# Two product orders and three moved tasks in a retention and mixture-of-experts kernel

## The chip, the cores and the metric

The kernel runs on one core of a Trainium2 chip. The core has a matrix engine (TensorE, PE in the profile, with its weight loads as PEld), VectorE (DVE), ScalarE (ACT), GpSimd (POOL) and SyncE (SP, which only issues DMAs here). The metric is the device time of one execution in microseconds. Lower is better. The time before is a median of three runs.

## The reference

A retention layer (8 sequences of 576 positions, 8 heads of 64) feeds a top-1 mixture of 8 experts, all in float32.

```python
ret = scale * (q @ k.T) * Dmat          # Dmat[i, j] = gamma ** (i - j), lower triangle
x = (ret @ v)                           # reshaped to N=4608 tokens of D=512
expert_idx = np.argmax(xn @ en.T / tau, axis=1)
gate_w = softmax(...)[chosen expert]
for e in range(8):
    mask = expert_idx == e
    h = np.maximum(x[mask] @ w1[e], 0.0)            # 512 -> 1024
    out[mask] = gate_w[mask, None] * (h @ w2[e])    # 1024 -> 512
```

## The kernel before

The first part of the program (up to about 170 us) computes the retention, routes every token to its expert and writes the token rows and the gates to DRAM. Then the experts follow one after the other. Each expert has room for 640 tokens, held as CT = 5 tiles of 128. A float32 operand is split into a high and a low part, and each product is made of three matmuls (high by high, high by low, low by high).

For experts 1 to 7 the **first product** (x @ w1) is done in blocks. A two-by-two block scheme with 7 products (numbered n = 1 to 7) stands in place of 8, for each of four column groups i = 0 to 3, so an expert has 28 **block products** `(n, i)`. Each is six matmuls of 128 rows by 288, 304 or 320 columns; the width is chosen at run time by how many tokens the expert has, which is why the built program holds each product three times behind branches (L1264, L1267), of which one is run. The tuple `ORDER` gives the order of the 28, and its place in that order is called k below (k = 1 is the first).

The sums of the scheme are made in PSUM. Products 1, 6, 7 and 4 of a column group all accumulate into one bank, `Y[i]`, in this order. After 1, 6 and 7 the function `follow` has ScalarE copy the running sum from the bank to SBUF (L1279), because the scheme needs each of these partial sums. So product 7 may not start to write the bank before the copy after product 6 has read it. Product 2 has a bank `W[i]` and products 5 and 3 share a bank `Z[i]`. VectorE adds `W` and `Z` onto the copies (L1275, `add`), ScalarE applies the relu (L1224) and VectorE makes the low part (L1217).

```python
if n in (1, 6, 7):
    nc.scalar.copy({1: ya, 6: yb, 7: yc}[n][:, :HC], Y[i][:, :HC])
```

The copies land in the tiles `ys[0]` to `ys[4]`. The same tiles hold the output rows of the expert before, so a copy also waits until GpSimd's scatter of those rows has been done.

The **second product** (h @ w2, function `mm2`, L1349) runs over the five tiles: 24 matmuls of 128 by 512 each, then ScalarE scales the rows by the gate (L1375) and GpSimd scatters them to the output (`put_rows`, L1309, an indirect DMA). The fifth tile of experts 1 to 6 is special (`fitted`): where at most 64 tokens are left for it, its rows are packed, and one pair of passes over the packed tile `ht` (a part of the tile `w0s`) replaces the three. `both_parts` makes that packing with four VectorE copies from `hs` (L1331). Where nothing is left, the tile is left out.

All other work is spread over these two stages by hand. `mm1_plan(e)` says which tasks are written after which block product k, and `mm2_plan(e)` which are written at which third of which tile (index 3 * tile + third). Every engine runs its own instructions strictly in the order in which they are written, and waits on semaphores for what it needs. The tasks that matter here:

- `gather_gates(n, a0, a1)`: GpSimd fetches the gates of tiles a0 to a1 of expert n from DRAM (L380, one indirect DMA for each tile). They are read first when the second product of expert n is scaled.
- `gather`: GpSimd fetches the token rows of the expert after next (L366).
- `xjoin`, `xsums`, `xhigh`, `xlow`: ScalarE and VectorE prepare the x blocks of the next expert during the second product (L415 on ScalarE; L426, L432, L433, L454 on VectorE).
- `w1sum`, `w1hi`, `w1lo`, `w2hi`, `w2lo`: the sums and splits of the weights (L1175, L1149, L1152).
- `add_low`: GpSimd scatters the rows of the packed tile a second time with an add (L1309, `sidx`), after k = 10.

Of the kernel before, what the change touches and what calls it, by code (L numbers as in the profile page):

```python
# [29 lines left out]
CT = 5  # L30
# [65 lines left out]
def retention_moe(ctx: ExitStack, tc: tile.TileContext, qk, kn, v0s, vs, w1, w2, head, cst, out):  # L96
# [263 lines left out]
    def fitted(e, i):  # L360
        return i == CT - 1 and 0 < e < NE - 1
# [189 lines left out]
    with ExitStack() as att:  # L551
# [3 lines left out]
        a1 = att.enter_context(tc.tile_pool(name="a1", bufs=1))  # L555
# [551 lines left out]
    with ExitStack() as moe:  # L1107
# [164 lines left out]
        def follow(n, i):  # L1272
# [23 lines left out]
                highs.append(settle(yb, i, 1))  # L1296

        ORDER = (
# [3 lines left out]
        )  # L1302
# [87 lines left out]
        def mm2_plan(e):  # L1390
            n = e + 1
            own, sums = slice(0, 1), slice(1, 3)
            if n == NE:
                return {0: [(count_beyond,)], 3: [(half_rows,)]}
            plan = {
                0: [(xjoin, n, 0)],
                1: [(xsums, n, 0), (xhigh, n, 0, own), (xlow, n, 0, own), (xjoin, n, 1), (w1sum, n, 0), (xhigh, n, 0, sums)],
                2: [(w1hi, n, 0, True), (xsums, n, 1), (xlow, n, 0, sums), (xhigh, n, 1, own), (w1lo, n, 0, True)],
                3: [(xjoin, n, 2), (xlow, n, 1, own), (xhigh, n, 1, sums)],
                4: [(w1hi, n, 0, False), (xsums, n, 2), (xlow, n, 1, sums), (w1lo, n, 0, False)],  # L1400
                5: [(xhigh, n, 2, own), (xjoin, n, 3), (xlow, n, 2, own), (xhigh, n, 2, sums)],
                6: [(w1sum, n, 1), (xhigh, n, 3, own), (xsums, n, 3), (w1hi, n, 1, True), (xjoin, n, 4)],
                7: [(w1lo, n, 1, True), (xlow, n, 3, own), (xhigh, n, 3, sums), (xsums, n, 4), (xlow, n, 2, sums)],
                8: [(xhigh, n, 4, own), (xlow, n, 4, own), (xlow, n, 3, sums), (xhigh, n, 4, sums), (w1hi, n, 1, False)],
                9: [(xlow, n, 4, sums), (w1lo, n, 1, False)],
                10: [(w1sum, n, 2)],
                11: [(w1hi, n, 2, True), (w1lo, n, 2, True)],
                12: [],
            }
            if n + 1 < NE:  # L1410
                for i in range(CT):
                    plan[(2, 4, 8, 9, 11)[i]].append((gather, n + 1, i))
            if fitted(e, CT - 1):
                plan[9].insert(1, (both_parts,))
            for k, a0, a1 in ((2, 0, 2), (5, 2, 4), (9, 4, CT)):
                plan[k].insert(0, (gather_gates, n, a0, a1))
            if n + 1 < NE:
                plan[12].append((xturn, n + 1, 0))
            if e == 0:
                plan[0] = [(xturn, 1, 4)] + plan[0]  # L1420
            return plan

        def mm1_plan(e):
            n = e + 1
            plan = {
                2: [(w2hi, e, 0)],
                3: [(w2lo, e, 0)],
                5: [(w1hi, e, 2, False)],
                6: [(w1lo, e, 2, False), (w1sum, e, 3)],
                12: [(w1hi, e, 3, True)],  # L1430
                13: [(w1lo, e, 3, True)],
                14: [(w1hi, e, 3, False)],
                15: [(w1lo, e, 3, False)],
                18: [(w2hi, e, 1)],
                19: [(w2lo, e, 1)],
                21: [(w2hi, e, 2)],
                22: [(w2lo, e, 2)],
            }
            if n < NE:
                plan[10] = [(xturn, n, 3)]  # L1440
                plan[16] = [(xturn, n, 1)]
                plan[24] = [(xturn, n, 2)]
                plan[28] = [(xturn, n, 4)]
            return plan
# [13 lines left out]
        for f, ps in zip(PAIRS, first):  # L1458
            mm1_out(f, 0, ps)

        plan = {
            4: [(w2hi, 0, 0)],
            5: [(w2lo, 0, 0)],
            6: [(xprep, 0, 3), (xprep, 0, 4), (gates_exp,)],
            7: [(w2hi, 0, 1)],
            8: [(gates_sum,), (w2lo, 0, 1)],
            9: [(w2hi, 0, 2), (gather, 1, 3), (gather, 1, 4)],
            10: [(gates_out,), (w2lo, 0, 2), (xturn, 1, 0)],
            11: [(w2hi, 0, 3)],
# [9 lines left out]
        for e in range(NE):  # L1479
            if e:  # L1480
                plan = mm1_plan(e)
                for k, (n, i) in enumerate(ORDER, 1):
                    product(e, n, i)
                    follow(n, i)
                    if k == 10 and fitted(e - 1, CT - 1):
                        add_low(e - 1)
                    if k < len(ORDER):
                        run_tasks(plan, k)
                highs.pop()()
                w2hi(e, 3)  # L1490
                lows.pop()()
                w2lo(e, 3)
                held.pop()()
                run_tasks(plan, len(ORDER))
            plan = mm2_plan(e)
            for i in range(CT):
                if (e, i) == (0, 2):
                    load_left()
                if e * CT + i == NA - 2:
                    ntile = nc.values_load(ovt[0:1, 0:1], min_val=0, max_val=NO)  # L1500
                mm2(e, i, lambda k: run_tasks(plan, 3 * i + k))
# [196 lines left out]
```

## Time and profile before

| | |
|---|---|
| median of three runs | 551.64 us (551.02 to 553.75) |
| the profiled execution | 551.17 us |
| its span, first to last instruction | 549.1 us |
| PE busy in the span | 541.6 us, 99% |
| PEld, DVE, ACT, POOL busy | 89%, 76%, 69%, 46% |
| granted TensorE clock | 1.000, all of the span |

The profiled execution takes 2.1 us more than its span, which is time ahead of the first and behind the last instruction. A busy share is an average over stages with different limits. TensorE's matmuls are pipelined and their ends are modelled, so a row can reach past the start of the next one. The time that matters is the distance from the start of one group of matmuls to the start of the next: what it holds beyond the usual pace of that group is a stall, also where the row shows a smaller idle time.

### The profile page before, as it was taken

To read this page: it belongs to the slowest core of one execution; us is meant where nothing else is said; L and a number is where in the kernel's file an instruction comes from. 1 tells how busy PE (TensorE), PEld (TensorE's weight loads), DVE (VectorE), ACT (ScalarE), POOL (GpSimd) and SP (SyncE) were. 2 spreads that over 40 slices of the span, in tenths; PEclk is the share of its full clock that TensorE was granted. 3 is DMA by queue.
4 is the path that set the end of the run, shared out by engine and by line. 5 is a ranking of instruction groups with operands and counts; after the bars stand their busy time and mean duration, and the time that the engine had idled before them with its cause. 6 is when DMAs were issued, how large, how long until landed. Compare 5 with 4: busy or idle time off the path is not lost. (4 is left out here: it accounts for less than half of the span.)

```text
span 549.1 us, 13547 instructions
## 1 busy us (share of the span) xinstructions
PE 541.6 (99%) x5051; PEld 489.4 (89%) x5051; DVE 419.9 (76%) x975; ACT 377.4 (69%) x700; POOL 250.9 (46%) x239
## 2 busy tenths in 40 slices
PE   9999999999999999999999999999999999999996
PEld 8898988989898899889988987998898899889985
DVE  4856788798876957995897889689888958976810
ACT  1257454547758859977896898789789868957511
POOL 6773435553463751285057318704731851334022
PEclk9999999999999999999999999999999999999999
DMA  9999999978458474847556655675665565632111
GB/s 325 407 383 369 371 330 356 378 275 274 160 186 206 161 203 117 166 146 185 159 167 168 164 163 175 183 159 161 184 164 157 173 174 154 137 135 64 66 39 50
DMA packets 81974, 109.79 MB, mean 200 GB/s; under 512 B 43094, under 2 KB 44538, under 8 KB 81888
## 3 DMA queue, kind: packets, MB, share of 16 engines
q1 hardware_dynamic: 71920, 86.24, 51.4%
q0 software_dynamic: 8560, 20.16, 11.9%
q10 hardware_dynamic: 1408, 2.17, 1.1%
q8 instruction: 63, 1.03, 0.7%
q14 instruction: 23, 0.19, 0.1%
HBM read 80.27 MB, written 21.51 MB: 185 GB/s over the span
## 5 line engine op out<-in xcount | busy, mean ns | idle before, releaser
L1349 PE MATMUL m<-w2s,hs 128*128 128x512 f32 x552 | 127.2, 389 | 0.0
L1349 PEld LDWEIGHTS m<-w2s,hs 128*128 128x128 f32 x552 | 103.4, 188 | 21.3
L1309 POOL DMA_INDIRECT out<-y,sid x41 | 45.7, 1115 | 166.1 <-ACT y L1375 134.1
L1349 PE MATMUL a<-w2s,hs 128*128 128x512 f32 (+1 forms) x360 | 78.8, 375 | 0.0
L1349 PEld LDWEIGHTS a<-w2s,hs 128*128 128x128 f32 x360 | 64.2, 188 | 11.9
L366 POOL DMA_INDIRECT raw<-xd,gid x40 | 42.9, 1073 | 19.4 <-issue 9.3
L1224 ACT ACTIVATE hs<-y 128x320 fp32r<-128x320 f32 x84 | 39.2, 473 | 13.1 <-DVE y L1275 12.5
L415 ACT COPY raw<-raw 128x1024 uint16<-128x1024 uint16 x35 | 47.7, 1363 | 0.0
L734 POOL TENSOR_TENSOR kt<-kt,cs 128x512 f32<-128x512 f32 x28 | 28.4, 1044 | 42.1 <-DMA kt<-kn 42.1
L380 POOL DMA_INDIRECT gt<-gd,gid x34 | 39.0, 1146 | 17.2 <-issue 9.7
L1152 DVE TENSOR_TENSOR w2s<-raw,w2s 128x1024 fp32r<-128x1024 f32 x32 | 39.1, 1222 | 8.3 <-ACT w2s L1149 8.2
L1275 DVE TENSOR_TENSOR y<-a,y 128x320 f32<-128x320 f32 x53 | 25.5, 486 | 26.0 <-issue 11.4
L1217 DVE SCALAR_TENSOR_TENSOR hs<-y,hs 128x320 fp32r<-128x320 f32 x84 | 42.3, 510 | 3.3 <-ACT hs L1224 1.3
L1255 PE MATMUL m<-xsb,w0s 128*128 128x288 f32 (+2 forms) x270 | 43.8, 300 | 0.1
L1255 PE MATMUL a<-xsb,w0s 128*128 128x288 f32 (+2 forms) x270 | 43.6, 301 | 0.2 <-ACT y L1279 0.2
L1255 PEld LDWEIGHTS a<-xsb,w0s 128*128 128x128 f32 x270 | 39.2, 188 | 0.4 <-ACT y L1279 0.4
L1255 PEld LDWEIGHTS m<-xsb,w0s 128*128 128x128 f32 x270 | 39.2, 188 | 0.3 <-DVE hs L1217 0.3
L1375 ACT ACTIVATE y<-m,gt 128x512 f32<-128x512 f32 x26 | 17.8, 686 | 31.0 <-PE m L1349 31.0
L408 ACT COPY raw<-raw 128x1024 uint16<-128x1024 uint16 x35 | 36.6, 1045 | 0.0
L1149 ACT CAST w2s<-raw 128x1024 fp32r<-128x1024 f32 x32 | 33.4, 1043 | 2.4 <-DMA raw<-w 2.4
L753 POOL TENSOR_TENSOR qkt<-qkt,gsb 128x384 f32<-128x384 f32 x32 | 31.3, 1008 | 6.5 <-issue 4.2
L454 DVE TENSOR_TENSOR xsb<-raw,xsb 128x128 fp32r<-128x128 f32 x70 | 30.4, 484 | 0.0
(274 smaller groups left out, 1216.9 us busy)
## 6 DMA issues: line engine op xcount, KB each, us to landing
raw<-w SPq DMA_DIRECT2D x64, 512.0 KB
qkt<-qk SPq DMA_DIRECT2D x28, 576.0 KB
xd<-y SPq DMA_DIRECT2D x36, 256.0 KB
vt<-vs SPq DMA_DIRECT2D x7, 1152.0 KB
kt<-kn SPq DMA_DIRECT2D x7, 1024.0 KB
qkt<-qk ACTq DMA_DIRECT2D x4, 288.0 KB
qkt<-qk SPq DMA_DIRECT2D x4, 288.0 KB
out<-y,sid POOLq DMA_INDIRECT x41
```

The lines of the kernel that those rows point to most:

```text
L366: nc.gpsimd.indirect_dma_start(out=t[:, XO : XO + DM], out_offset=None, in_=xd[:rows, :], in_offset=bass.IndirectOffsetOnAxis(ap=gid[:, a ...
L380: nc.gpsimd.indirect_dma_start(out=g[:, i : i + 1], out_offset=None, in_=gd[:, :], in_offset=bass.IndirectOffsetOnAxis(ap=ids, axis=0),)
L408: nc.scalar.copy(far.rearrange("p (h n) -> p h n", h=2), near.rearrange("p (n h) -> p h n", h=2))
L415: nc.scalar.copy(far.bitcast(U16).rearrange("p (n h) -> p h n", h=2), near.rearrange("p (h n) -> p h n", h=2))
L753: nc.gpsimd.tensor_tensor(out=q, in0=q, in1=gsb[:, p, :], op=ALU.mult)
L1149: nc.scalar.copy(hi, u)
L1152: nc.vector.tensor_tensor(out=lo, in0=u, in1=hi.bitcast(F32), op=ALU.subtract)
L1217: nc.vector.scalar_tensor_tensor(out=lo, in0=part(src), scalar=0.0, in1=hi.bitcast(F32), op0=ALU.max, op1=ALU.subtract)
L1224: nc.scalar.activation(hi, part(src), AF.Relu)
L1255: nc.tensor.matmul(ps[:, :n_cols], w[:, ws, ka, d * P : (d + 1) * P], xop(kx, xsp)[:, d, :n_cols], start=(n in (1, 2, 5) and d == 0 and k ...
L1309: put = nc.gpsimd.indirect_dma_start(out=out.rearrange("t (k n) -> (t k) n", k=k), out_offset=bass.IndirectOffsetOnAxis(ap=rows, axis=0), ...
L1349: nc.tensor.matmul(ps[:, :step], rows[f // NPR][:, f % NPR] if rows is ht else rows[:, f], w[:, ws, f, n : n + step], start=(m == 0), stop ...
```

## The change

```diff
         ORDER = (
-            (1, 0), (2, 0), (5, 0), (1, 1), (6, 0), (2, 1), (5, 1), (7, 0), (6, 1), (1, 2),
+            (1, 0), (2, 0), (5, 0), (1, 1), (2, 1), (5, 1), (6, 0), (7, 0), (6, 1), (1, 2),
...
             if fitted(e, CT - 1):
-                plan[9].insert(1, (both_parts,))
-            for k, a0, a1 in ((2, 0, 2), (5, 2, 4), (9, 4, CT)):
+                plan[0].append((both_parts,))
+            for k, a0, a1 in ((2, 0, 2), (5, 2, 4), (9, 4, CT))[1 if e else 0 :]:
                 plan[k].insert(0, (gather_gates, n, a0, a1))
...
             if n < NE:
                 plan[10] = [(xturn, n, 3)]
+                plan[11] = [(gather_gates, n, 0, 2)]
                 plan[16] = [(xturn, n, 1)]
```

Three things move; nothing is added or taken away.

**The order of the block products**, in all seven experts. `(6, 0)` goes from place 5 to place 7, behind `(2, 1)` and `(5, 1)`. The first six products now each start on a bank of their own. `(7, 0)` stays at place 8. On TensorE (last expert, the copies of 304 columns, with the semaphores of the engines that a row waits for; `a3` is the bank `Y[0]`, `m2` is `W[1]`, `m0` is `Z[1]`, `a1` is `Y[1]`) places 5 to 9 read before:

```order
L1255 MATMUL a3_67<-xsb_2531,wsa_2532 128x304 [waits Activation_49]
L1255 MATMUL a3_67<-xsb_2531,wsa_2532 128x304 x5
...
L1255 MATMUL m2_70<-xsa_94,w0s_89 128x304 x6
...
L1255 MATMUL m0_68<-xsb_2531,w0s_89 128x304 x2
L1255 MATMUL m0_68<-xsb_2531,w0s_89 128x304 [waits DVE_49]
L1255 MATMUL m0_68<-xsb_2531,w0s_89 128x304 x3
...
L1255 MATMUL a3_67<-xsb_2531,wsa_2532 128x304 [waits Activation_49]
L1255 MATMUL a3_67<-xsb_2531,wsa_2532 128x304 x5
...
L1255 MATMUL a1_65<-xsb_2531,w0s_89 128x304 x6
```

and with the change:

```order
L1255 MATMUL m2_70<-xsa_94,w0s_89 128x304 x6
...
L1255 MATMUL m0_68<-xsb_2531,w0s_89 128x304 [waits Activation_49]
...
L1255 MATMUL m0_68<-xsb_2531,w0s_89 128x304 [waits DVE_49]
L1255 MATMUL m0_68<-xsb_2531,w0s_89 128x304 x3
...
L1255 MATMUL a3_67<-xsb_2531,wsa_2532 128x304 [waits Activation_49]
L1255 MATMUL a3_67<-xsb_2531,wsa_2532 128x304 x5
...
L1255 MATMUL a3_67<-xsb_2531,wsa_2532 128x304 [waits Activation_49]
L1255 MATMUL a3_67<-xsb_2531,wsa_2532 128x304 x5
...
L1255 MATMUL a1_65<-xsb_2531,w0s_89 128x304 x6
```

The two products on bank `a3`, `(6, 0)` and `(7, 0)`, had two products of other banks between them and now follow each other. The wait of the second is for ScalarE's copy of the first.

On ScalarE the copies move along. At the same place in the last expert it had `y1` (the copy after `(1, 1)`), `y2` (after `(6, 0)`), the cast of `w1hi`, the relu of `y1` and `y0` (after `(7, 0)`):

```order
L1279 COPY y1_85<-a1_65 128x320 [waits DMASW1_49,PE_49]
L1279 COPY y2_86<-a3_67 128x320 [waits DMASW4_49,PE_49,Activation_49]
L1149 CAST w0s_89<-wsum_2534 128x1024
...
L1224 ACTIVATE hs_2530<-y1_85 128x5x64 [waits DVE_49]
L1279 COPY y0_84<-a3_67 128x320 [waits PE_49,Activation_49]
```

and it now has:

```order
L1279 COPY y1_85<-a1_65 128x320 [waits DMASW1_49,PE_49]
L1149 CAST w0s_89<-wsum_2534 128x1024
L1224 ACTIVATE hs_2530<-y1_85 128x5x64 [waits DVE_49]
L1279 COPY y2_86<-a3_67 128x320 [waits DMASW4_49,PE_49,Activation_49]
...
L1279 COPY y0_84<-a3_67 128x320 [waits PE_49,Activation_49]
```

The cast and the relu now stand ahead of the copy of `y2`.

**VectorE's row copies** (`both_parts`, experts 1 to 6) go from the fourth tile of the second product to the first third of the first tile. On VectorE, at the head of the second product of expert 1, behind the last low parts of the first product (`hs`) and ahead of the first sums of the next x (`raw`):

```order
 L1152 TENSOR_TENSOR w2s<-raw_77,w2s 128x1024
 L1217 SCALAR_TENSOR_TENSOR hs<-y_84,hs 128x5x64
+L1331 COPY w0s<-hs 128x8x32 x4
 L426 TENSOR_TENSOR raw_78<-raw_78 128x256
 L432 TENSOR_TENSOR raw_78<-raw_78 128x128
```

The four copies have been put between `hs` and the x sums.

**GpSimd's gathers of the first two gates** of experts 2 to 7 (two indirect DMAs each, twelve in all) go from the head of the second product to the block products ahead of it, after k = 11. The other three gates of an expert stay.

## Rows read from the trace of the kernel before

**Rows 1.** The page: busy time with its share of the span, and the clock.

```profile
PE 541.6 (99%) x5051; PEld 489.4 (89%) x5051; DVE 419.9 (76%) x975; ACT 377.4 (69%) x700; POOL 250.9 (46%) x239
...
PEclk9999999999999999999999999999999999999999
```

**Rows 2.** Waits on PE: total us, times, longest us.

```profile
PE m L1349 <- DVE w0s L1331: 0.4, 2, 0.2
...
PE a L1255 <- PEq L1369: 0.3, 1, 0.3
...
PE a L1255 <- ACT y L1279: 0.2, 1, 0.2
```

**Rows 3.** Busy time by stretch: the block products of expert 6.

```profile
442.50:465.90 23.40, 23.40 (x169) 23.40 (x168) 16.88 (x29) 19.34 (x36) 7.22 (x7) 1.00 0.62 166
```

**Rows 4.** Timeline of the last expert, places 5 to 9: start us, us.

```profile
496.49 0.99 PE L1255 MATMUL a<-xsb,wsa 128*128 128x304 f32 x6
496.69 0.43 ACT L1279 COPY y<-a 128x320 f32<-128x320 f32 x1 [0.62 <-PE a L1255]
...
497.32 1.00 PE L1255 MATMUL m<-xsa,w0s 128*128 128x304 f32 x6
497.56 0.43 ACT L1279 COPY y<-a 128x320 f32<-128x320 f32 x1 [0.45 <-PE a L1255]
497.88 1.05 ACT L1149 CAST w0s<-wsum 128x1024 fp32r<-128x1024 f32 x1
...
498.41 0.49 DVE L1275 TENSOR_TENSOR y<-m,y 128x320 f32<-128x320 f32 x1 [1.20 <-ACT y L1279]
...
498.93 0.47 ACT L1224 ACTIVATE hs<-y 128x320 fp32r<-128x320 f32 x1
...
498.99 0.99 PE L1255 MATMUL a<-xsb,wsa 128*128 128x304 f32 x6
...
499.82 1.00 PE L1255 MATMUL a<-xsb,w0s 128*128 128x304 f32 x6
```

**Rows 5.** Timeline of expert 5, places 7 to 9: start us, us.

```profile
395.46 1.04 PE L1255 MATMUL a<-xsb,w0s 128*128 128x320 f32 x6
...
396.19 0.43 ACT L1279 COPY y<-a 128x320 f32<-128x320 f32 x1 [1.11 <-PE m L1255]
...
396.67 1.15 PE L1255 MATMUL a<-xsb,w0s 128*128 128x320 f32 x6 [0.16 <-ACT y L1279]
...
397.65 0.31 PE L1255 MATMUL m<-xsb,w0s 128*128 128x320 f32 x1
```

**Rows 6.** Timeline of PE, second product of expert 3: tiles 2 to 5.

```profile
325.00 5.60 PE L1349 MATMUL a<-w2s,hs 128*128 128x512 f32 x24
330.44 11.04 PE L1349 MATMUL m<-w2s,hs 128*128 128x512 f32 x48
341.64 1.66 PE L1349 MATMUL m<-w2s,w0s 128*128 128x512 f32 x6 [0.16 <-DVE w0s L1331]
```

**Rows 7.** Timeline of POOL: expert 5's second product, and one row of expert 2's.

```profile
422.84 1.01 POOL L1309 DMA_INDIRECT out<-y,sid  x1 [18.70 <-ACT y L1375]
424.15 1.02 POOL L380 DMA_INDIRECT gt<-gd,gid  x1 [0.30 <-issue]
425.48 1.20 POOL L380 DMA_INDIRECT gt<-gd,gid  x1 [0.30 <-issue]
...
292.07 1.06 POOL L366 DMA_INDIRECT raw<-xd,gid  x1 [0.30 <-issue]
```

**Rows 8.** Timeline of VectorE: head of expert 6's second product, the copies in two experts.

```profile
469.21 0.48 DVE L1217 SCALAR_TENSOR_TENSOR hs<-y,hs 128x320 fp32r<-128x320 f32 x1
470.27 0.43 DVE L426 TENSOR_TENSOR raw<-raw 128x256 f32<-128x256 f32 x1 [0.57 <-ACT raw L415]
...
486.78 0.89 DVE L1331 CAST w0s<-hs 128x256 fp32r<-128x256 f32 x4
...
292.21 1.05 DVE L1331 CAST w0s<-hs 128x256 fp32r<-128x256 f32 x4
```

## The prediction

> **What bounds the kernel now.** I read the page first. TensorE is busy for 541.6 us of the span, 99%, at full granted clock in every slice [rows 1]. So whatever another engine does counts only where it makes TensorE wait, and the question for each edit is which wait of TensorE it ends or begins. Next come TensorE's waits. From the first block product on there are three kinds: twice 0.2 us for the packed rows (L1331), 0.3 us at a branch where expert 4's fifth tile is left out, and 0.2 us for one of ScalarE's copies (L1279) [rows 2]. The table by stretch says the same of a whole stage: in the block products of expert 6 TensorE is busy for 23.40 of 23.40 us, while GpSimd works for 7.22 [rows 3]. There is very little to win: these waits are 0.9 us together, and about 2 us when each is measured by the distance of the groups, as below; that is 0.4% of the time.
>
> The timelines then give the true size of a stall. In expert 3's second product 24 matmuls take 330.44 - 325.00 = 5.44 us, so the next 48 should end at 341.32; the packed tile starts at 341.64 [rows 6]: 0.32 us late. Expert 5 shows what comes on top. Six matmuls from 395.46 on take 0.88 us at the pace of 320 columns, so the next product was due at 396.34. It starts at 396.67, and takes 0.98 us instead of 0.88, since the pipeline has to fill again [rows 5]. I count 0.10 us of refill behind every stall: 0.42 us for the packed tile, 0.43 us in expert 5.
>
> **The order of the products.** This is the edit that touches TensorE itself. Before, the copy of `Y[0]` after `(6, 0)` had the time of two products of other banks before `(7, 0)` needed it. Now it has none: `(7, 0)` writes the same bank, is next in a queue that runs strictly in order, and carries the wait for that copy. So in each of the seven experts TensorE has to stand still from the end of `(6, 0)` until ScalarE has read it. The last expert shows every piece of that time [rows 4]:
>
> - `(6, 0)` ends, by the start of the next product, at 497.32. Its copy starts at 497.56: 0.24 us from the last matmul to ScalarE. (For the copy after `(1, 1)`, which ends at 496.49, it is 0.20.)
> - The copy takes 0.43 us.
> - From its end to TensorE's next matmul: 0.05 us (396.19 + 0.43 = 396.62, matmul at 396.67) [rows 5].
> - Refill: 0.10 us.
>
> That is 0.82 us in each expert, and 7 x 0.82 = 5.7 us. Nothing covers it, because no other matmul stands ahead of `(7, 0)` in the queue.
>
> It holds only if ScalarE is free when `(6, 0)` ends. With the change a cast and a relu stand ahead of the copy. In the last expert: the copy after `(1, 1)` ends at 497.12, the cast of 1.05 us follows at once and ends near 498.2. The relu waits for VectorE's add of `(2, 1)`, which can start 0.25 us after that product's end. `(2, 1)` now ends where `(6, 0)` ended, 497.32, so the add runs from about 497.6 to 498.1, and the relu (0.47 us) from 498.2 to 498.65. `(6, 0)` ends two products later, at 497.32 + 2 x 0.835 = 498.99, and its copy is due at 499.23 [rows 4]. ScalarE is free 0.6 us too early, so 0.82 stands. Expert 5 is the exception: there the copy after `(6, 0)` came only at 396.19, behind 1.11 us of idle time which I can't explain [rows 5]. Now `(6, 0)` itself would end at 396.34, so a repeat of this lateness costs from nothing up to some 1.1 us. I take nothing.
>
> What does the order give back? The six products on banks of their own no longer need any copy for 5 us. But the wait that this takes away, `(6, 0)` for the copy after `(1, 0)`, does not show among the waits [rows 2]. The wait of 0.43 us in expert 5 is the one of `(7, 0)`, and is replaced by the new one. So the order costs 5.7 - 0.43 = 5.3 us.
>
> **VectorE's row copies.** They are 0.89 us of work [rows 8]. At the old place they come last before the packed tile, and the tile waits for them in two experts, 2 and 3. At the new place they are done four tiles earlier, so both stalls go: 2 x 0.42 = 0.85 us saved. At the head VectorE had 0.57 us of idle time, waiting for ScalarE [rows 8], so the x sums behind the copies start 0.3 us later; they are wanted at the end of the second product, and VectorE gets back 0.89 us there. No loss.
>
> **The gate gathers.** Two gathers are 1.02 + 1.20 us and two gaps of 0.30, 2.8 us of GpSimd's queue [rows 7]. At the head of the second product it shortens the queue by that much, and the token gathers and scatters behind them come 2.8 us earlier. Who waits for these? ScalarE's copies into the `ys` tiles, and TensorE behind them; but TensorE's only wait for a copy is the one of expert 5. At the new place GpSimd has been idle for 18.70 us before the next scatter [rows 7], and the gates are read first when the second product's first tile ends, over 10 us later. Worth 0, up to 0.4 if the branch or another stray stall goes.
>
> A rule of the page "SBUF — State Buffer" of the Trainium skill, section "Who interferes with whom", speaks against both moves: VectorE and GpSimd share a pair of ports, taken as an exclusive lock, so a VectorE copy and the making of a GpSimd DMA's descriptors block each other. In this trace the four copies take 0.89 us alone and 1.05 us where a gather of 292.07 to 293.13 lies over them [rows 7, 8]. By the rule each overlap would cost the length of the other instruction, about 1 us; by the row it is 0.16 us, on engines that TensorE doesn't wait for. The sum goes by the row.
>
> **The sum**, on the profiled execution: 551.17 + 5.3 - 0.85 = 555.6 us. The median of the runs is 0.47 us above that execution, so I predict 556.0 us, 0.8% slower. About 0.5% (2.8 us) is what a measurement of this kernel can tell from no change.
>
> **The rivals.**
>
> 1. *The new wait is hidden or isn't there, and only the gains are left.* Then 0.85 + 0.43 = 1.3 us are saved: 550.3 us, not slower. For it: six products without any wait give ScalarE time to be early. Against it: the copy takes 0.43 us however early ScalarE is free, and it can't begin before the product's end. This rival decides once the wait costs less than 1.3 / 7 = 0.19 us an expert, under half of the copy alone.
> 2. *ScalarE is late at the copy.* If VectorE's add holds the relu ahead of the copy, or the lateness of expert 5 becomes the rule, it starts some 0.5 us later in each expert: 7 x 0.5 = 3.5 us more, 559.5 us. The 0.6 us of slack above speak against it; narrower products (0.80 us) leave about 0.1.
> 3. *The moved gathers hold VectorE.* Two in a row last 2.2 us [rows 7]. If VectorE's sums in the block products stood still that long in six experts, and half of it reached TensorE, this would add 6.7 us: 562.7 us. The overlap of 0.16 us speaks against it.
> 4. *The wait is cheaper than its pieces*, about 0.5 us, because ScalarE's start or the refill overlaps: 7 x 0.5 - 1.3 = 2.2 us, 553.8 us, within 0.5%.
>
> **How the numbers follow.** The forecast has a chance of 0.71 and a range of its own from 554.6 (other stray stalls gone too) to 557.3 (expert 5's lateness on top). Rival 1 has 0.08, rival 2 0.10, rival 3 0.03, rival 4 0.08. The range that holds the time 8 times in 10 leaves out rival 1, rival 3 and the upper half of rival 2: 553.6 to 558.8 us. Slower by over 0.5% (above 554.4) is the forecast but for 0.03 of it, and rivals 2 and 3: 0.81. Within 0.5% is the rest of these, and rival 1: 0.17. Faster by over 0.5% has 0.02: all of TensorE's stalls of this part together are less than that.
>
> **What the new profile would show.** Right: a wait of `a` L1255 for ScalarE's `y` L1279 in all seven experts, one product each time, starting 1.5 to 1.6 us after the product before it instead of 0.8; seven experts' block products longer by 0.8 us each (expert 5's by 0.4); no wait for L1331; the second products of experts 2 and 3 shorter by 0.4 us. GpSimd's two gathers lie behind `add_low`, and its scatters come earlier with no effect on TensorE. Wrong: `(7, 0)` starting within 0.3 us of its usual pace (rival 1), ScalarE's copy starting later than 0.3 us after `(6, 0)` (rival 2), or VectorE rows above 1 us beside the moved gathers with TensorE waiting on VectorE (rival 3).

## The result, and the profile after

| | before | after |
|---|---|---|
| median, measured together, six runs each | 551.21 us | 555.3 us |
| ratio, 95% interval | | 1.0063, 1.0038 to 1.0088 |
| the profiled execution | 551.17 us | 553.21 us |
| from the first matmul of expert 0's second product to the end of TensorE's last matmul | 373.73 us | 377.81 us |

The change makes the kernel 4.1 us slower; 556.0 us was predicted, in a range of 553.6 to 558.8. The profiled execution is the fastest of its six: the unchanged part ahead of that first matmul took 168.81 us in it and 170.62 us in the profiled one of before. So the last line of the table, called **the stretch** below, is the better measure of a profile: it leaves out the part that the change doesn't touch, and it grew by 4.08 us.

The page of the kernel after, busy time and clock ([rows 1] before):

```profile
PE 540.7 (98%) x5051; PEld 489.0 (89%) x5051; DVE 418.5 (76%) x975; ACT 377.6 (68%) x700; POOL 251.1 (46%) x239
...
PEclk9999999999999999999999999999999999999999
```

TensorE's waits after ([rows 2] before: total us, times, longest us):

```profile
PE a L1255 <- ACT y L1279: 3.9, 7, 0.6
...
PE a L1255 <- PEq L1369: 0.3, 1, 0.3
```

The wait for ScalarE's copy is there seven times instead of once, the wait for the packed rows (L1331) is gone. The table by stretch, block products of expert 6 ([rows 3] before):

```profile
443.12:467.38 24.26, 23.70 (x170) 23.45 (x169) 16.70 (x29) 19.36 (x36) 7.63 (x8) 1.00 0.55 148
```

The stage had no gap and now has one of 0.56 us; it is 24.26 us long instead of 23.40, so 0.30 us more are lost than the gap shows. Where they are is seen in the timeline of the last expert, places 6 to 9 ([rows 4] before):

```profile
498.15 0.43 ACT L1279 COPY y<-a 128x320 f32<-128x320 f32 x1 [0.62 <-PE a L1255]
498.47 1.05 ACT L1149 CAST w0s<-wsum 128x1024 fp32r<-128x1024 f32 x1
498.79 1.00 PE L1255 MATMUL m<-xsb,w0s 128*128 128x304 f32 x6
499.57 0.47 ACT L1224 ACTIVATE hs<-y 128x320 fp32r<-128x320 f32 x1
499.62 0.99 PE L1255 MATMUL a<-xsb,wsa 128*128 128x304 f32 x6
500.69 0.43 ACT L1279 COPY y<-a 128x320 f32<-128x320 f32 x1 [0.65 <-PE a L1255]
...
501.17 1.10 PE L1255 MATMUL a<-xsb,wsa 128*128 128x304 f32 x6 [0.56 <-ACT y L1279]
502.10 0.72 PE L1255 MATMUL a<-xsb,w0s 128*128 128x304 f32 x4
```

Read the starts. `(6, 0)` at 499.62 should end at 500.45 (its pace is 0.835 us). The copy begins 0.24 us later, at 500.69, and takes 0.43; `(7, 0)` starts at 501.17, 0.72 us late, and takes 0.93 us instead of 0.83 to 0.84. The row itself shows an idle time of only 0.56 us. Place 7 lasts 1.55, 1.51, 1.52, 1.51, 1.60, 1.56 and 1.55 us in the seven experts, place 8 is 0.10 us longer in each. Expert 5 ([rows 5] before) is now like the others:

```profile
394.80 1.92 PE L1255 MATMUL a<-xsb,w0s 128*128 128x320 f32 x12
396.80 0.43 ACT L1279 COPY y<-a 128x320 f32<-128x320 f32 x1
397.28 1.15 PE L1255 MATMUL a<-xsb,w0s 128*128 128x320 f32 x6 [0.56 <-ACT y L1279]
398.27 0.90 PE L1255 MATMUL m<-xsb,w0s 128*128 128x320 f32 x5
```

And the second product of expert 3 ([rows 6] before), with VectorE's row copies at their new place in expert 6 ([rows 8] before):

```profile
330.25 11.05 PE L1349 MATMUL m<-w2s,hs 128*128 128x512 f32 x48
341.13 3.90 PE L1349 MATMUL m<-w2s,w0s 128*128 128x512 f32 x16
```

```profile
471.07 0.89 DVE L1331 CAST w0s<-hs 128x256 fp32r<-128x256 f32 x4
```

48 matmuls take 10.88 us from start to start, and the packed tile follows without a gap. The second products of experts 2 and 3 last 0.47 and 0.41 us less. The account of the stretch: seven stalls of about 0.82 us, +5.76; expert 5's old stall, -0.43; a stray stall in expert 3's block products that did not come back, -0.38; the packed tile, -0.88: in all +4.07 us, against 4.08 measured.

### The profile page after: what moved, and what is told of

It is laid out like the page before. It is cut to its first block, busy times and chain, and to the rows that moved or that the text cites. A ratio compares the mean times of both kernels' runs of the same rounds, so it can differ in the third digit from the quotient of the medians.

```text
span 551.4 us, 13535 instructions
## 1 busy us (share of the span) xinstructions
PE 540.7 (98%) x5051; PEld 489.0 (89%) x5051; DVE 418.5 (76%) x975; ACT 377.6 (68%) x700; POOL 251.1 (46%) x239
## 4 chain that ended last, share of the span: by engine, by line
PE 84%; DMA 8%; DVE 2%; issue 2%; ACT 2%; POOL 1%; POOLq 0%; SPq 0%; ACTq 0%
PE m L1349 21%; PE a L1255 13%; PE m L1255 12%; PE a L1349 12%; DMA out<-y,sidx 7%; PE a L763 3%; PE a L846 2%; PE m L763 2%; PE m L465 2%; PE a L465 2%; PE m L846 2%; PE m L929 1%; PE a L929 1%; PE m L790 1%; PE a L790 1%
## 5 line engine op out<-in xcount | busy, mean ns | idle before, releaser
L366 POOL DMA_INDIRECT raw<-xd,gid x40 | 48.9, 1223 | 28.2 <-DVE xsb L454 12.8
L1275 DVE TENSOR_TENSOR y<-a,y 128x320 f32<-128x320 f32 x53 | 25.5, 485 | 29.2 <-ACT y L1279 25.4
L1217 DVE SCALAR_TENSOR_TENSOR hs<-y,hs 128x320 fp32r<-128x320 f32 x84 | 40.4, 488 | 6.5 <-ACT hs L1224 4.5
L408 ACT COPY raw<-raw 128x1024 uint16<-128x1024 uint16 x35 | 36.6, 1045 | 0.0
```

The costliest lines, as they stand in the source:

```text
L366: nc.gpsimd.indirect_dma_start(out=t[:, XO : XO + DM], out_offset=None, in_=xd[:rows, :], in_offset=bass.IndirectOffsetOnAxis(ap=gid[:, a ...
L408: nc.scalar.copy(far.rearrange("p (h n) -> p h n", h=2), near.rearrange("p (n h) -> p h n", h=2))
L1217: nc.vector.scalar_tensor_tensor(out=lo, in0=part(src), scalar=0.0, in1=hi.bitcast(F32), op0=ALU.max, op1=ALU.subtract)
```

## The experiments

Ratios are to the kernel before on the same chip, with 95% intervals. "Stray" is a stall of TensorE in the profile that no step of the prediction names.

| kernel | ratio | interval | stretch, us |
|---|---|---|---|
| the change | 1.0063 | 1.0038 to 1.0088 | 377.8 |
| order_only | 1.0102 | 1.0077 to 1.0127 | 379.0 |
| parts_only | 1.0056 | 1.0035 to 1.0077 | 376.5 |
| gates_only | 1.0026 | 1.0009 to 1.0043 | 376.2 |
| parts_gates | 0.9991 | 0.9973 to 1.0010 | 372.4 |
| one_between | 0.9988 | 0.9963 to 1.0012 | 378.7 |
| banks_apart | 1.0001 | 0.9975 to 1.0028 | 374.7 |
| second_pair | 1.0284 | 1.0250 to 1.0318 | 390.5 |
| late_cast | 1.0118 | 1.0084 to 1.0152 | 381.0 |
| short_copy | 1.0037 | 1.0020 to 1.0053 | 376.1 |
| parts_turn | 0.9987 | 0.9973 to 1.0000 | 373.1 |
| both_turn | 0.9989 | 0.9967 to 1.0011 | 373.1 |
| parts_turn22 | 1.0021 | 1.0001 to 1.0041 | 375.6 |

### Each part by itself

**order_only**: the kernel before with the new `ORDER`.

> The kernel before with only the new order of the block products. If the whole loss is the wait of (7, 0) for the copy after (6, 0): 7 x 0.82 less 0.43 of expert 5's old stall = 5.3 us slower than before (about 556.6, ratio 1.0096), with the two waits for L1331 of 0.2 us each still there, and places 7 and 8 longer by 0.72 and 0.10 us in every expert. The stretch from the first matmul of expert 0's second product to the end, 373.73 us before, then takes about 379.0 us. If the moved gathers or row copies share in the loss, this kernel loses clearly less than 4.5 us.

TensorE's waits from the experts on:

```profile
PE a L1255 <- ACT y L1279: 3.6, 6, 0.8
PE a L1255 <- ACT hs L1224: 0.7, 1, 0.7
PE m L1349 <- DVE w0s L1331: 0.4, 2, 0.2
```

The stretch is 379.0 us as expected, 5.3 more than before (strays changed it by a few tenths both ways: expert 3's went, experts 5 and 7 lost 0.15 and 0.28 us more than 0.82). The order alone makes the whole loss.

**parts_gates**: the change with the old `ORDER`.

> The changed kernel with the old order of the block products. If the order holds the whole loss: 0.85 us faster than before, up to 1.3 us if a stray stall goes with it (about 550.0 to 550.5, ratio 0.9976 to 0.9985); no block product of places 7 and 8 longer than its pace except in expert 5 (0.43 us), stretch 372.5 to 372.9 us. If the gathers or the row copies take part in the loss, it is slower than before.

In the experts only the wait at the branch is left among the waits of TensorE that the profile lists; a stall of 0.4 us behind place 14 of expert 4, a stray, shows only in the distances. The stretch is 372.4 us, 1.3 less than before, and by the ratio the time is 0.5 us less, within the measurement. Against this kernel the order costs 5.4 us in the stretch.

**parts_only** and **gates_only**: the kernel before with one of the two moves.

```diff
-                plan[9].insert(1, (both_parts,))
+                plan[0].append((both_parts,))
```

> The kernel before with only the row copies at the head of the second product. By the prediction both stalls ahead of a packed tile go, 2 x 0.42 = 0.85 us faster than before, stretch about 372.9 us, second products of experts 2 and 3 at 25.7 us instead of 26.1, nothing else moved. If the copies at the head hold up VectorE's sums for the next x, or collide with the gathers there, part of it is given back at the start of the next block products, and the stretch stays within 0.3 us of 373.7.

```diff
-            for k, a0, a1 in ((2, 0, 2), (5, 2, 4), (9, 4, CT)):
+            for k, a0, a1 in ((2, 0, 2), (5, 2, 4), (9, 4, CT))[1 if e else 0 :]:
...
+                plan[11] = [(gather_gates, n, 0, 2)]
```

> The kernel before with only the twelve gate gathers moved into the block products. By the prediction no change: stretch 373.3 to 373.8 us (0.4 us less at most, if a stray stall goes). If the gathers hold VectorE in the block products, six experts' block products get longer by some tenths of a us each: stretch above 375 us.

Both missed. In parts_only the second products of experts 2 and 3 take 25.5 us each, 0.4 to 0.5 less than before, as expected, and yet the kernel is 3.1 us slower. It loses 1.9 us in the block products of expert 4 and 1.5 in expert 5. gates_only loses 1.7 and 0.5 us in the same stages, and 0.2 us in each of two second products, where the packed rows come later still. When both are moved, all that is left of these losses is the 0.4 us in expert 4. The places are told apart in the timeline of parts_only, expert 5, places 7 and 8, where `(7, 0)` starts 1.55 us late:

```profile
397.85 1.04 PE L1255 MATMUL a<-xsb,w0s 128*128 128x320 f32 x6
399.01 0.43 ACT L1279 COPY y<-m 128x320 f32<-128x320 f32 x1 [2.28 <-PE a L1255]
399.80 0.43 ACT L1279 COPY y<-a 128x320 f32<-128x320 f32 x1 [0.36 <-PE a L1255]
...
400.28 1.15 PE L1255 MATMUL a<-xsb,w0s 128*128 128x320 f32 x6 [1.38 <-ACT y L1279]
```

and expert 4, places 14 and 15:

```profile
356.84 0.96 PE L1255 MATMUL m<-xsa,w0s 128*128 128x288 f32 x6
358.92 1.07 PE L1255 MATMUL a<-xsb,w0s 128*128 128x288 f32 x6 [1.13 <-issue]
```

In expert 5 ScalarE idles for 2.28 us and waits for TensorE's semaphore, of a product that ended at 396.08. In expert 4 TensorE waits for nothing that the profile shows; the matmul carries no semaphore wait in the program. Both are taken up in the last section.

### The wait itself

**one_between** and **banks_apart**: the change with one product of another bank between the pair.

```diff
-            (1, 0), (2, 0), (5, 0), (1, 1), (2, 1), (5, 1), (6, 0), (7, 0), (6, 1), (1, 2),
+            (1, 0), (2, 0), (5, 0), (1, 1), (2, 1), (6, 0), (5, 1), (7, 0), (6, 1), (1, 2),
```

> The changed kernel with (6, 0) at place 6, so that one product of another bank, (5, 1), stands between (6, 0) and (7, 0). By the pieces the wait is 0.24 + 0.43 + 0.05 = 0.72 us and a product lasts 0.80 to 0.88 us: the wait is covered, and the loss of the order goes altogether, to the level of the old order with the same other moves (550.7 us), within what stray stalls do (1 us). If the cost comes from six products on own banks in a row, or from ScalarE being late as such, some of the 5 us stays: 552 to 555 us.

```diff
-            (1, 0), (2, 0), (5, 0), (1, 1), (2, 1), (5, 1), (6, 0), (7, 0), (6, 1), (1, 2),
+            (1, 0), (2, 0), (5, 0), (1, 1), (2, 1), (5, 1), (6, 0), (6, 1), (7, 0), (1, 2),
```

> The changed kernel with the first six products still on own banks, and (6, 1) drawn ahead of (7, 0): (6, 0), (6, 1), (7, 0). The bank rule of the change is kept, the adjacent pair is gone. By the theory of the pair: no wait for L1279, 550.7 us within 1 us. If the six own banks themselves cost something: about 555 us as with the change.

Both are back at the time of before. In one_between places 7 and 8 keep their pace in experts 2, 6 and 7; in the other four the pair still waits, for 0.35 to 1.21 us. One product covers the 0.72 us with only 0.08 to 0.16 to spare, and TensorE's semaphore updates came late there (last section): in expert 5 by 1.37 us, of which 0.16 are covered, and 1.21 were lost. Its profiled execution also met a stall of 2.1 us behind place 14 of expert 4, so its stretch says little. In banks_apart, where six products start on own banks as in the change, waits at place 8 of experts 1 and 4 cost 1.4 us, in stages with late updates; beside them there are only small stalls, 0.04 to 0.19 us, most with 0.10 of refill, in experts 2 to 5. So own banks cost nothing; the adjacent pair does.

**second_pair**: a second pair on one bank.

```diff
-            (4, 0), (3, 0), (7, 1), (2, 2), (5, 2), (4, 1), (6, 2), (1, 3), (2, 3), (7, 2),
+            (4, 0), (3, 0), (7, 1), (2, 2), (5, 2), (4, 1), (1, 3), (2, 3), (6, 2), (7, 2),
```

> The changed kernel with a second adjacent pair on one bank in each expert: (6, 2) stands directly ahead of (7, 2), at places 19 and 20. By the theory each pair costs 0.82 us in each of seven experts: 5.7 us more than the change (about 561.0 us), and the place of (6, 2) lasts 1.5 to 1.6 us like that of (6, 0). If the cost of the change is something else about the start of the block products, about 555.3 us.

The wait came, at twice the price: the stretch is 12.7 us longer than the change's, and the new pair costs 1.4 to 1.9 us in each expert. Expert 4, from place 19 on:

```profile
368.21 0.96 PE L1255 MATMUL m<-xsb,w0s 128*128 128x288 f32 x6
369.07 0.43 ACT L1279 COPY y<-a 128x320 f32<-128x320 f32 x1 [0.62 <-DVE hs L1217]
369.39 1.05 ACT L1149 CAST w2s<-raw 128x1024 fp32r<-128x1024 f32 x1
370.33 0.43 ACT L1279 COPY y<-m 128x320 f32<-128x320 f32 x1
...
370.82 1.07 PE L1255 MATMUL m<-xsb,w0s 128*128 128x288 f32 x6 [1.65 <-ACT y L1279]
```

`(6, 2)` ends at 369.01 and its copy is due at 369.25, but a cast of `w2` stands ahead, itself behind a copy that waited for VectorE. The copy starts at 370.33, 1.08 us late: 0.72 + 1.08 = 1.80 us, and 1.81 are measured. The expectation counted neither ScalarE's tasks ahead of the copy nor their waits. This is rival 2's mechanism, at a place where ScalarE has no slack.

**late_cast**: the dose of that rival at the place of the change.

```diff
-                5: [(w1hi, e, 2, False)],
-                6: [(w1lo, e, 2, False), (w1sum, e, 3)],
+                6: [(w1hi, e, 2, False), (w1lo, e, 2, False), (w1sum, e, 3)],
```

> The changed kernel with ScalarE's cast of w1hi (1.05 us) written after place 6 instead of 5, directly ahead of the copy after (6, 0). ScalarE was idle for 0.58 to 0.67 us ahead of that copy; the relu ahead of the cast ends at about 0.4 us before the end of (6, 0), so the cast should now end some 0.4 us after the copy was due (0.33 to 0.44 by the width). If the stall is the time from the end of (6, 0) to the end of ScalarE's copy, it grows by as much: 7 x 0.4 = 2.8 us more than the change, about 558 us. If ScalarE has more slack than that, or TensorE waits for something else, 555.3 us.

3.2 us more than the change in the stretch, 3.0 by the ratios; but not evenly: 0.17 to 0.34 us in experts 1, 2, 6 and 7, 0.65 to 0.82 in experts 3, 4 and 5. Experts 3 and 4 also show late updates, and in expert 5 ScalarE had only 0.04 us of idle time ahead of this copy in the change, against 0.6 in the others. So the cast's delay does reach TensorE, but that the total is near the 2.8 us expected is partly luck. The last expert:

```profile
504.06 0.99 PE L1255 MATMUL a<-xsb,wsa 128*128 128x304 f32 x6
504.39 1.03 ACT L1149 CAST w0s<-wsum 128x1024 fp32r<-128x1024 f32 x1
505.32 0.42 ACT L1279 COPY y<-a 128x320 f32<-128x320 f32 x1
...
505.79 1.09 PE L1255 MATMUL a<-xsb,wsa 128*128 128x304 f32 x6 [0.74 <-ACT y L1279]
```

ScalarE's rows overlap by 0.1 us (the cast ends at 505.42, the copy begins at 505.32), so each step ahead of the copy is worth 0.1 us less than its row. The copy is 0.19 us late, TensorE 0.18.

**short_copy**: a shorter copy after `(6, 0)`; the other 288 columns of that partial sum are left out.

```diff
-                nc.scalar.copy({1: ya, 6: yb, 7: yc}[n][:, :HC], Y[i][:, :HC])
+                c = 32 if (n, i) == (6, 0) else HC
+                nc.scalar.copy({1: ya, 6: yb, 7: yc}[n][:, :c], Y[i][:, :c])
```

> The changed kernel with ScalarE's copy after (6, 0) cut from 320 to 32 columns (the other columns of that partial sum are left out, so column group 0's second half is not computed). A copy of 64 columns takes 0.234 to 0.252 us before, one of 320 0.426, so about 0.21 us for 32. If the stall is the copy with its latencies, place 7 gets shorter by 0.21 to 0.22 us in each expert, 1.3 instead of 1.51 to 1.56 us, 7 x 0.215 = 1.5 us in all (the stretch from the first second product to the end 376.3 instead of 377.8 us, plus stray stalls). If TensorE stands still for a fixed time because two products on one bank follow each other, whatever ScalarE does, place 7 stays at 1.51 to 1.56 us.

```profile
499.99 0.99 PE L1255 MATMUL a<-xsb,wsa 128*128 128x304 f32 x6
501.06 0.18 ACT L1280 COPY y<-a 128x32 f32<-128x32 f32 x1 [0.65 <-PE a L1255]
...
501.30 1.09 PE L1255 MATMUL a<-xsb,wsa 128*128 128x304 f32 x6 [0.32 <-ACT y L1280]
```

The copy takes 0.18 us, 0.25 less, and place 7 lasts 1.31 us in this expert, 1.27 to 1.36 in all: 0.24 less in each. The stretch is 1.7 us shorter. The stall follows the copy.

### The stray stalls

**parts_turn**, **both_turn** and **parts_turn22**: parts_only, parts_gates, and parts_only again, each with the transpose of the next expert's first x tile moved from the start of the block products to k = 20, 20 and 22.

```diff
-            if n + 1 < NE:
-                plan[12].append((xturn, n + 1, 0))
...
+                plan[20] = [(xturn, n, 0)]
```

> Only the row copies moved (554.7 us, 3.7 us slower than before, with 2.9 us of stray stalls in the block products of experts 4 and 5), and in addition the DMA transpose that is issued at the start of each block product stage moved to k = 20. If that transpose, beside a weight load and GpSimd's scatters and gathers, makes TensorE's semaphore updates and its code loads late, the stray stalls of places 7 to 15 in experts 4 and 5 go, and the time falls to 550 to 551.5 us. If the row copies themselves cost the time, or the crowd is one of the other transfers, it stays at 554 to 555 us.

> The old order with the row copies and the gathers moved as in the change (550.7 us), and the same transpose moved to k = 20. If the transpose makes the stray stalls: 549 to 550.3 us, and the runs lie closer together than the 4.0 us (548.7 to 552.8) that they had. If not: 550.7 us with the same spread.

> As the kernel with the row copies moved and the transpose at k = 20, but the transpose at k = 22. At k = 20 ScalarE's reordering copy of 1.05 us stood ahead of the copy after (6, 3), and (7, 3) waited for that in experts 2 to 4: place 23 lasted 1.05 us instead of 0.80, and place 24 0.90. At k = 22 it stands behind that copy, so 3 x 0.35 = 1.05 us go: stretch 372.0 instead of 373.1 us, against 373.7 before, ratio about 0.997. If the early transpose makes the stray stalls, there are again none at places 4 to 15, and TensorE's semaphore updates come 0.17 us after the product's end throughout. If the run before was only spared by chance, experts 4 and 5 lose 1 to 3 us again (554 us).

parts_turn is 3.8 us faster than parts_only, relative to before, and the early strays are gone. both_turn gained nothing and spread as widely as parts_gates (548.9 to 552.7 us). parts_turn22 came out slower (1.0021, where 0.997 was expected): the reordering copy (L408) left the copy after `(6, 3)` and now stands ahead of the one after `(7, 3)`, for which `(4, 3)` waits at place 27. Expert 4, from place 25 on:

```profile
365.23 0.96 PE L1255 MATMUL m<-xsb,w0s 128*128 128x288 f32 x6
365.68 1.04 ACT L408 COPY raw<-raw 128x1024 uint16<-128x1024 uint16 x1
...
366.95 0.41 ACT L1279 COPY y<-a 128x320 f32<-128x320 f32 x1
...
367.42 1.85 PE L1255 MATMUL a<-xsb,wsa 128*128 128x288 f32 x12 [0.43 <-ACT y L1279]
```

That costs 0.7 us in three experts and 0.2 in three, and expert 5 lost 0.9 us at places 15 and 19. What made the strays of parts_only is not settled by this: these three kernels and short_copy ran on another chip than the eight kernels above them, and short_copy is free of them too, with the transpose at its old place.

## Why the prediction was right, point by point

- **The new wait, 0.82 us in each expert.** Right in size and in each piece: 0.24 to the copy, 0.43 of copy, 0.05 back, 0.10 of refill. The length of the copy (short_copy), one product between (one_between, banks_apart) and a delay ahead of the copy (late_cast) each move the stall as the pieces say.
- **The sum.** Its terms add up to 4.45 us in the stretch (and to 556.1 us, not 556.0); 4.08 were measured. The difference is expert 3's stray of 0.38 us, which the prediction didn't count and which was gone after the change; why is not known, so that part is luck.
- **ScalarE is free in time.** Right: 0.58 to 0.67 us of idle time ahead of the copy in six experts, 0.6 forecast, and 0.58 in the three with the narrowest products. In expert 5 the relu ahead waited 0.45 us for VectorE's add, as rival 2 feared, and 0.04 us of idle time was left. That was just enough.
- **Rivals 1 and 4** (hidden, or cheaper) are out. **Rival 2** is out for this place in the change and true for another, in second_pair. **Rival 3** is out: the gathers hold nothing. After the change, with VectorE's low part (L1217) beside a gate gather:

```profile
457.05 0.96 POOL L380 DMA_INDIRECT gt<-gd,gid  x1 [0.30 <-issue]
457.13 0.88 DVE L1217 SCALAR_TENSOR_TENSOR hs<-y,hs 128x320 fp32r<-128x320 f32 x2
```

  Two of them take 0.88 us, 0.44 each, as by themselves. Of the 112 in the experts 20 lie beside one of GpSimd's DMAs and none of its sums, and none of these takes more than 0.49 us.
- **The row copies save 0.85 us.** Right in the change: 0.88. By themselves they saved as much in the second products, but the kernel came out 3.1 us slower (parts_only), for a reason that the prediction didn't have: strays.
- **The gates are worth nothing.** Together with the row copies, yes. By themselves they cost 1.4 us, again in strays; the sum of the three single ratios would be 1.8%, not 0.6%. The terms were priced one by one as if they added up, and that step holds for the stalls in the program's order, not for these.
- **Expert 5's lateness**, left unexplained and taken at nothing: it did not recur in the change's profile, and that was luck. In second_pair, whose order is the same up to place 16, TensorE's update for the copy after `(6, 0)` came 0.59 us late in expert 5, and `(7, 0)` started 1.30 us late there instead of 0.72. What is known of it stands below.

## What to carry to other kernels

Between two writes of one PSUM bank with a read in between, leave other work on the writing engine that lasts longer than the whole round trip, here 0.72 us against products of 0.80 to 0.88. One product is enough on paper; two also cover an update that comes late, here by up to 1.05 us at the widest product. Before moving a product, look at what stands ahead of the reader's instruction in its own queue, waits included: a pair on one bank cost 0.82 us at one place and 1.4 to 1.9 at another. And price a move by its profile in the company of the other moves, since the strays here did not add.

## What the hardware showed that was not expected

**TensorE's semaphore updates can come late, and then in a burst.** In the change every update of a block product that the trace holds comes 0.16 to 0.19 us after the product's end (the start of the next). Elsewhere it does not. Expert 5, from the trace's semaphore records (us):

```
parts_only  (5,0)   (1,1)   (6,0)   (2,1)   (5,1)
end        395.19  396.08  396.96  397.85  398.73
update     395.40  398.99  399.73  399.81  399.88
before     (5,0)   (1,1)   (6,0)
end        392.80  393.69  394.57
update     393.10   394.63   396.12
```

The copy after `(6, 0)` started 0.07 us behind that update in both. In the order of before, this copy can be 1.05 us late before `(7, 0)` waits (two products of 0.88 us less 0.71 for the copy and the steps around it). The update is 2.60 us late in parts_only (2.77 less 0.17) and 1.38 in before: stalls of 1.55 and 0.33 us follow, and 1.55 and 0.33 are measured. In gates_only the update is 1.91 us late, and the stall 0.87. The late update of before is the idle time of 1.11 us in [rows 5]. Late updates lie at places 1 to 8 of experts 1 to 5, with few exceptions, in before and in the eight profiles from order_only to late_cast; there are none in the change and in the last four kernels of the table. In parts_only the packets of GpSimd's DMAs from 395.5 on took up to 2.4 us then, against at most 0.7 in before; but in gates_only, whose update is later than that of before, they took at most 0.9. What holds the updates up was not found; the chip is not ruled out either, since the four kernels that are free of them beside the change all ran on one chip.

**TensorE stands still behind a late load of code.** The stall behind place 14 of expert 4 without a wait, against the packets of an instruction queue (q8 on the page, 16 KB each):

```
             load ended   next product   after
parts_only     357.46        358.92       1.46
gates_only     357.83        359.31       1.48
parts_gates    353.13        354.57       1.44
one_between    356.82        358.29       1.47
before         354.91        356.62       1.71   (no stall)
banks_apart    355.48        357.22       1.74   (no stall)
short_copy     356.18        357.73       1.55   (no stall)
```

In the four stalled runs TensorE goes on 1.44 to 1.48 us behind the load's end; where the load was done earlier, by 1.55 us or more in the other ten, there is no stall. That the load holds TensorE is argued from these times, not shown by an edit.

**VectorE beside GpSimd's sums.** L1217 takes 0.48 us alone. Beside GpSimd's own sums (L1175) in parts_only:

```profile
354.90 0.99 POOL L1175 TENSOR_TENSOR wsum<-raw 128x256 f32<-128x256 f32 x1
355.21 1.02 DVE L1217 SCALAR_TENSOR_TENSOR hs<-y,hs 128x320 fp32r<-128x320 f32 x1
```

Ten of the seventeen that overlap such a sum by more than 0.05 us there take more than 0.6 us. The Trainium skill, page "SBUF — State Buffer", section "Who interferes with whom", says that a VectorE instruction with two SBUF inputs contends with a GpSimd instruction that reads SBUF. The trace agrees for GpSimd's sums (1.02 against 0.48 us), and shows nothing of it for GpSimd's DMAs alone (at most 0.49). No row copy overlapped a gather in the change, so the rule weighed in the prediction was not put to the test there.
